# Moving two start-up loads of a fused attention and MLP kernel to the sync queue: wk's last chunks between x2 and x3, and x of group 1 behind x3

## The chip, the cores and the metric

One core of a Trainium2 chip. The metric is the device time of one execution in microseconds (us). A profile's span is 1.7 to 2.1 us shorter than the time of the same execution. All times inside a trace below count from the start of its span. Runs that are compared are "fast" (granted TensorE clock about 1.0) unless the text says otherwise. A single untimed look has the state "unknown".

## The reference

Two branches read the layer norm of the same `x` (2048 tokens, 640 features), and their sum is added to `x`:

```python
xn = layernorm(x)                                   # per token, over 640 features
# branch A: linear attention, 32 heads of 20
q, k, v = split(xn @ wqkv)                          # wqkv 640 x 1920
pq, pk = phi(q), phi(k)                             # phi(t) = t + 1 if t > 0 else exp(t)
o = (pq @ (pk^T @ v)) / (pq . sum(pk))              # per head
A = o @ wo
# branch B
B = gelu(xn @ w1 + b1) @ w2 + b2                    # 640 -> 1536 -> 640
out = x + A + B
```

## The kernel before

The tokens are 16 tiles of 128 (x0 to x15); a group is four tiles. `wk` is the middle third of `wqkv`, in five chunks of 128 rows. Only the start matters here. The loads stand first:

```python
    def load_x(t0, t1, queue=nc.sync):
        queue.dma_start(out=x_all[:, t0:t1, :], in_=xv[:, t0:t1, :])

    def load_wk(k0, k1):
        nc.scalar.dma_start(out=wqk[:, k0:k1, D : 2 * D], in_=wqkv_v[:, k0:k1, D : 2 * D])

    load_x(0, 1)                 # sync (SP) queue
    load_x(1, 2, nc.scalar)      # scalar (ACT) queue
    load_x(2, 3)
    load_x(3, 4)
    # ... cut ...
    load_wk(0, 3)                # ACT queue
    load_wk(3, NC)               # ACT queue; NC = 5
    load_x(4, 8, nc.scalar)      # group 1, four tiles
```

Each partition holds 16 consecutive tokens, so one tile of x is 1280 contiguous bytes of a partition, and x4 to x7 together are 5120 contiguous bytes. A chunk of wk is 1280 bytes of a partition.

The loads of w1, Q's weights and x8 to x15 stand on the sync queue and are held back by a memset on VectorE that follows the statistics of x1 (cut). Then comes the compute, in program order for each engine:

```python
    nc.scalar.preload_act_table_set("natural_log_exp_and_others")
    emit_warm(10)                # ten matmuls on constants, before any data is there
    emit_stats(0)                # VectorE: bn_stats of two halves of 320 columns, then bn_aggr
    emit_center(0)               # VectorE: x0 - mean (its rstd is applied later)
    emit_T_first(0, ((0, 3, nc.scalar.copy), (3, NC, nc.scalar.copy)))   # PE, copies on ScalarE
    emit_warm(1)
    emit_stats(1)
    emit_later_loads()
    emit_stats(2)
    emit_rstd(0, 2)              # ScalarE: Ln, Exp
    emit_norm(1)                 # VectorE
    emit_Ka(0)                   # PE: K of x0, five matmuls over the chunks of wk
    emit_rstd(2, 3)
    emit_T_first(1, ((0, 3, nc.scalar.copy), (3, NC, nc.scalar.copy)))
    emit_stats_half(3, 0)
    emit_norm(2)
    emit_stats_half(3, 1)
    emit_Kb(0)
    emit_T(2, nc.vector.tensor_copy, (0, 3, NC))
    emit_Ka(1, 0, 3)
    # ... cut: K of x1, x2, x3 ...
    for j in range(NJ):
        emit_h(0, j)             # PE: h = xn @ w1, the first long unbroken piece of TensorE work
        # ... cut ...
```

The lines of the profile that recur: L342 and L352 are the matmuls of K, L286 the transposes of x0 and x1, L261 the transposes of x2 and x3, L530 the matmuls of h, L227 the statistics, L247 the norm.

## Time and profile before

| | before |
|---|---|
| time, median of 3 runs | 196.26 us (196.21 to 197.03) |
| span of the profiled run | 194.4 us |
| PE busy | 188.7 us, 97% |
| first matmul of h | 13.57 us |

TensorE (PE) is the bottleneck. Lines of the page: the busy times, and the head of the chain that ended last.

```profile
PE 188.7 (97%) x1229; PEld 111.2 (57%) x1240; DVE 163.3 (84%) x392; ACT 89.8 (46%) x165; POOL 21.3 (11%) x54
...
PE 94%; DMA 3%; ACTq 0%; issue 0%; DVE 0%
```

Read: to the end of the kernel hardly anything but matmuls stands in the chain. What can still be moved is the moment at which the unbroken work begins. The chain in order of time (start, length, what) shows which load is in it:

```profile
1.73 5.83 DMA wqk<-in_A_wqkv_dram
7.56 0.04 issue
7.60 0.59 PE bank_169 L342 x2
8.19 0.17 PE bank_177 L286 x3
8.36 0.11 PE bank_182 L286 x2
8.47 0.28 PE bank_191 L352 x5
8.75 0.33 PE bank_197 L261 x5
```

It is wk's second piece, chunks 3 and 4. The timeline of PE at the same place (start, busy us, what, and in brackets the idle time before it with what ended it):

```profile
6.39 0.82 PE L342 MATMUL bank_169<-wqk,xnT 128*128 128x512 bf16 x3 [0.24 <-ACT xnT L290]
7.60 0.59 PE L342 MATMUL bank_169<-wqk,xnT 128*128 128x512 bf16 x2 [0.39 <-DMA wqk<-in_A_wqkv_dram]
8.03 0.33 PE L286 MATMUL bank_177<-identity,xn 128*128 128x128 bf16 x3
8.20 0.27 PE L286 MATMUL bank_182<-identity,xn 128*128 128x128 bf16 x2
8.31 0.44 PE L352 MATMUL bank_191<-wqk,xnT 128*128 128x128 bf16 x5
8.63 0.45 PE L261 MATMUL bank_197<-identity,xn 128*128 128x128 bf16 x5
```

The first K product does three chunks, waits 0.39 us for the load, and does the last two. That wait is what the change goes for. VectorE (DVE) is without a pause there. These are its lines around the two norms (L247) that the next transposes need:

```profile
7.43 0.40 DVE L247 TENSOR_SCALAR xn<-x_all,mv,rstd 128x640 bf16<-128x640 bf16 x1
7.74 0.49 DVE L227 BATCH_NORM_STATS2 stats<-x_all 128x6 f32<-128x320 bf16 x1
8.14 0.43 DVE L247 TENSOR_SCALAR xn<-x_all,mv,rstd 128x640 bf16<-128x640 bf16 x1
```

The norm of x2 ends at 8.14 + 0.43 = 8.57, and its transpose (L261) starts at 8.63. So there are two things that can hold the transpose of x2, at almost the same moment: the load, through PE's own order, and VectorE's chain.

### The profile page before, as it was taken

The page shows a single profiled execution, that of the slowest core. Times are in us where ns is not written, and L with a number is a line of the kernel's source. Part 1 is how long each engine was busy: PE and PEld are TensorE (multiplying, and loading weights), DVE is VectorE, ACT ScalarE, POOL GpSimd, SP SyncE. Part 2 cuts the span into 40 slices and gives each one's busy share as a digit, 9 for nine tenths or more (in the row PEclk, how much of TensorE's full clock was granted, in tenths as well). Part 3 has the DMA queues.
Part 4 walks back from the last instruction along what each step waited for, and adds up shares of the span by engine and source line. Part 5 has one row for each costly group of instructions (what it writes and reads, how often), then busy time and mean ns, then how long its engine had stood idle before and what let it go on. Part 6 is the DMA issues. An engine that isn't in the chain of part 4 may idle for free.

```text
span 194.4 us, 3333 instructions
## 1 busy us (share of the span) xinstructions
PE 188.7 (97%) x1229; PEld 111.2 (57%) x1240; DVE 163.3 (84%) x392; ACT 89.8 (46%) x165; POOL 21.3 (11%) x54
## 2 busy tenths in 40 slices
PE   8799999999999999999999999999999999999993
PEld 2464444544445454444445777767777777777772
DVE  2978969999699998696878999899999999777442
ACT  2569676558679688899795230050011010110100
POOL 1004170003239100002400100000000000000000
PEclk9999999999999999999999999999999999999999
DMA  6999735944343000000009885300201021010112
GB/s 196 347 251 348 279 81 107 343 182 100 102 122 84 0 0 2 0 0 3 0 4 230 290 245 172 112 0 2 71 0 67 0 71 58 11 67 3 67 58 77
DMA packets 24447, 20.19 MB, mean 104 GB/s; under 512 B 11120, under 2 KB 24048, under 8 KB 24432
## 3 DMA queue, kind: packets, MB, share of 16 engines
q1 hardware_dynamic: 23328, 18.20, 30.8%
q10 hardware_dynamic: 1104, 1.80, 2.5%
q8 instruction: 9, 0.15, 0.3%
q14 instruction: 6, 0.05, 0.1%
HBM read 12.78 MB, written 5.24 MB: 93 GB/s over the span
## 4 chain that ended last, share of the span: by engine, by line
PE 94%; DMA 3%; ACTq 0%; issue 0%; DVE 0%
DMA wqk<-in_A_wqkv_dram 3%; PE bank_1282 L884 2%; PE bank_1273 L884 2%; PE bank_1209 L851 2%; PE bank_2112 L1037 1%; PE bank_2028 L1037 1%; PE bank_1944 L1037 1%; PE bank_1860 L1037 1%; PE bank_1771 L1037 1%; PE bank_1682 L1037 1%; PE bank_1556 L1037 1%; PE bank_1434 L1037 1%; PE bank_1398 L884 1%; PE bank_1386 L884 1%; PE bank_1510 L1037 1%; PE bank_1580 L1037 1%
## 5 line engine op out<-in xcount | busy, mean ns | idle before, releaser
L1037 PEld LDWEIGHTS <-xn 128*128 128x128 f16 x198 | 19.0, 98 | 7.2
L530 PEld LDWEIGHTS <-w_91 128*128 128x128 bf16 x120 | 11.7, 98 | 13.9
L227 DVE BATCH_NORM_STATS2 stats<-x_all 128x6 f32<-128x320 bf16 x32 | 13.7, 469 | 2.9 <-DMA x_all<-in_A_x_dram 2.9
L518 PEld LDWEIGHTS <-wqk 128*128 128x128 bf16 x100 | 9.7, 98 | 11.1
L342 PEld LDWEIGHTS <-xnT 128*128 128x128 bf16 x80 | 7.2, 98 | 7.3 <-issue 0.7
L884 PEld LDWEIGHTS <-xn 128*128 128x128 bf16 (+1 forms) x80 | 7.8, 98 | 3.0
L247 DVE TENSOR_SCALAR xn<-x_all,mv,rstd 128x640 bf16<-128x640 bf16 x16 | 6.2, 436 | 3.7 <-POOL rstd L243 3.6
L946 DVE TENSOR_TENSOR pqT<-pqT,xnT 128x256 bf16<-128x256 bf16 (+1 forms) x30 | 8.5, 328 | 0.0
L682 PEld LDWEIGHTS <-w_91 128*128 128x128 bf16 (+1 forms) x48 | 4.6, 97 | 5.6 <-issue 0.3
L352 PEld LDWEIGHTS <-xnT 128*128 128x128 bf16 x80 | 5.8, 98 | 3.5
L1052 PEld LDWEIGHTS <-Sq 128*128 128x128 f16 x66 | 6.3, 98 | 2.5 <-DVE Sq L937 0.2
L451 DVE TENSOR_TENSOR x_all<-x_all,b2b 128x640 bf16<-128x640 bf16 x16 | 7.0, 480 | 0.0
L190 POOL TENSOR_SCALAR_AFFINE_SELECT emask<-emask 128x160 int8<-128x160 int8 (+3 forms) x20 | 6.7, 346 | 0.9
L302 DVE TENSOR_SCALAR pqT<-pqT 128x512 bf16<-128x512 bf16 x20 | 5.7, 285 | 0.6 <-ACT pqT L299 0.6
L1052 PEld LDWEIGHTS <-pqT 128*128 128x128 bf16 x50 | 4.8, 98 | 1.8
L1037 PEld LDWEIGHTS <-hT_79 128*128 128x128 bf16 x48 | 4.7, 98 | 1.7
L1037 PEld LDWEIGHTS <-hT_80 128*128 128x128 bf16 x48 | 4.7, 98 | 1.7
L1132 ACT CAST late<-bank_1486 128x320 bf16<-128x320 f32 x1 | 0.4, 425 | 10.4 <-PE bank_1489 L1128 10.4
L216 PE MATMUL bank_124<-const-bfloat16-1.0 128*128 128x512 bf16 x10 | 4.2, 605 | 0.8 <-PEq L1280 0.8
L937 DVE TENSOR_TENSOR Sq<-pqT 128x256 f16<-128x256 bf16 x16 | 4.3, 284 | 0.0
L783 DVE TENSOR_TENSOR pk<-pk,GT 128x512 bf16<-128x512 bf16 x10 | 4.2, 422 | 0.0
L682 PEld LDWEIGHTS <-wv 128*128 128x128 f16 x24 | 2.2, 97 | 3.2 <-issue 0.7
(647 smaller groups left out, 508.5 us busy)
## 6 DMA issues: line engine op xcount, KB each, us to landing
xnT<-rec_rows SPq DMA_DIRECT2D x20, 128.0 KB, 2.6
out_dram<-late SPq DMA_DIRECT2D x14, 160.0 KB, 1.8
w_91<-in_B_w_dram SPq DMA_DIRECT2D x2, 960.0 KB, 7.8
w_93<-in_B_w_dram SPq DMA_DIRECT2D x3, 640.0 KB, 7.9
x_all<-in_A_x_dram SPq DMA_DIRECT2D x2, 640.0 KB, 8.5
wqk<-in_A_wqkv_dram SPq DMA_DIRECT2D x1, 800.0 KB, 8.1
wv<-in_A_wqkv_dram SPq DMA_DIRECT2D x1, 800.0 KB, 6.3
woA<-in_A_wo_dram SPq DMA_DIRECT2D x5, 160.0 KB, 3.0
```

The costliest lines, as they stand in the source:

```text
L190: nc.gpsimd.affine_select(out=out, in_=out, compare_op=ALU.is_ge, fill=0.0, base=base, pattern=pattern, channel_multiplier=sign)
L227: nc.vector.bn_stats(out=st[:, half, :], in_=x_all[:, t, half * HALF : (half + 1) * HALF])
L247: nc.vector.tensor_scalar(out=xn[:, t, ds], in0=x_all[:, t, ds], scalar1=mv[:, t, 0:1], scalar2=rstd[:, t : t + 1], op0=ALU.subtract, op1= ...
L342: nc.tensor.matmul(K_ps[t][:], lhsT=xnT[:, k, t * P : (t + 1) * P], rhs=wqk[:, k, D : D + TOK], start=(k == 0), stop=(k == NC - 1),)
L451: nc.vector.tensor_tensor(out=x_all[:, t, :], in0=x_all[:, t, :], in1=b2b[:], op=ALU.add)
L518: nc.tensor.matmul(ps[:], lhsT=wqk[:, k, m * P : (m + 1) * P], rhs=xnT[:, k, gs], start=(k == 0), stop=(k == NC - 1),)
L530: nc.tensor.matmul(ps[:], lhsT=w1[:, k, j * P : (j + 1) * P], rhs=xnT[:, k, g * TOK : (g + 1) * TOK], start=(k == 0), stop=(k == NC - 1),)
L682: nc.tensor.matmul(self.ps[name][:], lhsT=left[:, c, js], rhs=x_block(*block, c) if block else Tx({4: 3, 5: 0, 6: 1, 7: 2}[p], c), start=( ...
L884: nc.tensor.matmul(ps if len(right.shape) == 3 else ps.rearrange("p (c n) -> p c n", c=NC), lhsT=left[:, t, self.i], rhs=right[:, t], star ...
L946: nc.vector.tensor_tensor(out=pqT[:, c, gs], in0=pqT[:, c, gs], in1=xnT[:, c, gs], op=ALU.mult)
L1037: nc.tensor.matmul(self.ps[name][:, cols], lhsT=left[:, j], rhs=right[:, j, cols], start=(start and j == 0), stop=False, skip_group_check= ...
L1052: nc.tensor.matmul(self.ps[name][:, cols], lhsT=left[:, c], rhs=right[:, c, cols], start=False, stop=(stop and c == CH - 1), skip_group_ch ...
```

## The change

Its intent: wk's last chunks go ahead of x3, so that the first K product finds them. x4 to x7 follow behind x3 on the sync queue, and no wait is added to hold them back ("ungated").

```diff
-    def load_wk(k0, k1):
-        nc.scalar.dma_start(out=wqk[:, k0:k1, D : 2 * D], in_=wqkv_v[:, k0:k1, D : 2 * D])
+    def load_wk(k0, k1, queue=nc.scalar):
+        queue.dma_start(out=wqk[:, k0:k1, D : 2 * D], in_=wqkv_v[:, k0:k1, D : 2 * D])

     load_x(0, 1)
     load_x(1, 2, nc.scalar)
     load_x(2, 3)
+    load_wk(3, NC, nc.sync)
     load_x(3, 4)
+    load_x(4, 8)
 ... (cut)
     load_wk(0, 3)
-    load_wk(3, NC)
-    load_x(4, 8, nc.scalar)
```

The compute instructions and their order on PE, VectorE, ScalarE and GpSimd are the same in both kernels.

## The prediction

> **What bounds the kernel now.** The page gives PE 188.7 of 194.4 us busy (97%). The chain of waits is PE 94%, DMA 3%: one DMA, the second piece of wk (chunks 3 and 4, 320 KB), then matmuls back to back to the end. So only the first 14 us can move.
>
> **The start, from the timeline and the landings of the DMA issues (us).**
>
> | load | queue, issued | landed | first needed | slack |
> |---|---|---|---|---|
> | x0 | SP 0.81 | 3.85 | stats 3.87 | 0 |
> | x1 | ACT 0.80 | 4.08 | 5.34 | 1.3 |
> | wk chunks 0-2 | ACT 1.23 | 5.87 | 6.39 | 0.5 |
> | x2 | SP 1.25 | 4.40 | 6.38 | 2.0 |
> | x3 | SP 1.71 | 6.18 | 7.74 | 1.5 |
> | wk chunks 3-4 | ACT 1.73 | 7.56 | about 7.2 | -0.39 |
> | x4-7 | ACT 2.27 | 9.18 | 13.22 | 4.0 |
> | w1, first half | SP 6.51 | 12.97 | 13.52 | 0.55 |
>
> The one late load is wk 3-4: PE waits 0.39 us for it at 7.60. VectorE has no such hole: from x0's landing until 9.67 it never waits for a DMA.
>
> **What the change does.** It adds no compute and no bytes. wk 3-4 goes ahead of x3, x4-7 move from the ACT to the SP queue. The transfers still share the same engines: the windows show about 390 GB/s at 4 to 5 us, and 387 at 9 to 10 us, where the SP queue works alone. That agrees with the Trainium skill, "DMA: Bandwidth & Descriptors", "Issuing engines are not separate DMA queues"; I expect no bandwidth, only another order. Between 4.0 and 4.5 us no packet of SP's queue moves, although x3 was issued at 1.71; the transfers go nearly in order of issue.
>
> wk 3-4 now has 1280 KB up to its end instead of 1440: 160 KB at 390 GB/s is 0.4 us (estimate), so it lands at about 6.7 to 7.15 and the 0.39 us wait goes. x3 takes the place that wk 3-4 had, 1440 KB, so lands at about 7.5 instead of 6.2: 0.2 us before VectorE wants it. wk 0-2 may land up to 0.4 later (6.3), still before 6.39. x4-7 land at about 9.2 as before; w1's first half about 13.0.
>
> **How much is critical.** Little. After the wait, the transposes of x1 need its norm (VectorE, 7.43 to 7.83; weight load at 7.88, itself waiting for it), matmuls at 8.03: at most 0.11 us comes forward. Then the transpose of x2 needs the norm that ends at 8.57, and starts at 8.63 already. So the wait of 0.39 us turns into waits on VectorE, which this change does not move. Left over: 0.02 to 0.1 us out of 196. ScalarE's table load comes 1 us earlier, for nothing: its first work, at 5.86, waits for PE.
>
> **Prediction:** 196.2 us, 195.7 to 196.9; faster by over 2%: 0.01, within 2%: 0.97, slower: 0.02.
>
> **What would show it right.** The DMA wait of PE at 7.6 is gone; transposes of x1 near 7.92, of x2 at 8.6 again, now released by VectorE; first matmul of h (w1) at 13.5 within 0.1 of 13.57; the chain of waits passes through DVE and x0 instead of wk.
>
> **What would make it wrong.** x3 later than 7.8: VectorE's third-tile statistics stand before the norm of x2, so PE is late by the same amount (0.1 to 0.5 us slower). wk 0-2 later than 6.39. w1's first half behind x4-7 on the same queue later than 13.5. The runs before spread by 0.8 us, more than the effect; nothing here reaches 2% (3.9 us).

## The result

| | before | change |
|---|---|---|
| time, 6 runs each | 196.38 us (195.99 to 197.03) | 196.36 us (196.07 to 196.47) |
| ratio, with 95% interval | | 0.9992 (0.9973 to 1.0011) |
| span of the profiled run | 194.4 us | 194.4 us |

A ratio is the mean time of one kernel's fast runs over that of the other's of the same rounds, so not quite the ratio of the medians. The change is worth nothing that the runs resolve. In the trace it did what it was meant to do. Landing times (us, the completion of each load in the trace's DMA records):

| load | before | change | needed at |
|---|---|---|---|
| x0 | 3.85 | 3.81 | at once |
| wk chunks 0-2 | 5.87 | 5.70 | 6.4 |
| wk chunks 3-4 | **7.56** | **6.57** | 7.2 |
| x3 | **6.18** | **6.99** | 7.7 |
| x4 to x7 | 9.18 | 8.57 | 13.2 |
| w1, first half | 12.97 | 11.87 | 13.5 |

PE's timeline after the change, the lines that answer to those of before:

```profile
6.51 1.25 PE L342 MATMUL bank_169<-wqk,xnT 128*128 128x512 bf16 x5
7.84 0.34 PE L286 MATMUL bank_177<-identity,xn 128*128 128x128 bf16 x3
8.02 0.28 PE L286 MATMUL bank_182<-identity,xn 128*128 128x128 bf16 x2
8.13 0.44 PE L352 MATMUL bank_191<-wqk,xnT 128*128 128x128 bf16 x5
8.59 0.45 PE L261 MATMUL bank_197<-identity,xn 128*128 128x128 bf16 x5
```

The five matmuls of the first K product now run in one piece. The transposes of x1 come 0.19 us sooner (8.03 to 7.84), but the transpose of x2 only 0.04 (8.63 to 8.59). The weight loads of TensorE (PEld) say what they waited for:

```profile
7.83 0.28 PEld L286 LDWEIGHTS <-xn 128*128 128x128 bf16 x5 [0.57 <-DVE xn L247]
8.07 0.32 PEld L352 LDWEIGHTS <-xnT 128*128 128x128 bf16 x5
8.58 0.28 PEld L261 LDWEIGHTS <-xn 128*128 128x128 bf16 x5 [0.19 <-DVE xn L247]
```

Both transposes wait for VectorE's norms (L247). VectorE's own lines stand where they stood, 0.04 us sooner, as x0 landed 0.04 sooner:

```profile
7.39 0.40 DVE L247 TENSOR_SCALAR xn<-x_all,mv,rstd 128x640 bf16<-128x640 bf16 x1
7.70 0.49 DVE L227 BATCH_NORM_STATS2 stats<-x_all 128x6 f32<-128x320 bf16 x1
8.10 0.43 DVE L247 TENSOR_SCALAR xn<-x_all,mv,rstd 128x640 bf16<-128x640 bf16 x1
```

And the chain has changed its head. The load of wk is gone from it; x0 and VectorE are in it:

```profile
0.81 3.00 DMA x_all<-in_A_x_dram
3.81 0.02 issue
3.83 0.90 DVE stats L227 x2
...
7.26 0.21 DVE mv L229
7.47 0.32 DVE xn L247
7.79 0.05 issue
7.84 0.34 PE bank_177 L286 x3
```

The first matmul of h starts at 13.51 instead of 13.57 us. From there to the end of the span both traces take 180.86 us. The matmuls, compared one by one, are 0.06 to 0.07 us earlier in the change than before, from 9.8 us to the last.

### The profile page after: what moved, and what is told of

Same layout as the page of the kernel before. It is cut to its first block, busy times and chain, and to the rows that moved or that the text cites. A ratio compares the mean times of both kernels' runs of the same rounds, so it can differ in the third digit from the quotient of the medians.

```text
span 194.4 us, 3333 instructions
## 1 busy us (share of the span) xinstructions
PE 189.4 (97%) x1229; PEld 111.4 (57%) x1240; DVE 163.3 (84%) x392; ACT 89.8 (46%) x165; POOL 21.7 (11%) x54
## 3 DMA queue, kind: packets, MB, share of 16 engines
HBM read 12.78 MB, written 5.24 MB: 93 GB/s over the span
## 4 chain that ended last, share of the span: by engine, by line
PE 94%; DVE 2%; DMA 2%; issue 1%
PE bank_1282 L884 2%; PE bank_1273 L884 2%; PE bank_1209 L851 2%; DMA x_all<-in_A_x_dram 2%; PE bank_2112 L1037 1%; PE bank_2028 L1037 1%; PE bank_1944 L1037 1%; PE bank_1860 L1037 1%; PE bank_1771 L1037 1%; PE bank_1682 L1037 1%; PE bank_1556 L1037 1%; PE bank_1434 L1037 1%; DVE stats L227 1%; PE bank_1398 L884 1%; PE bank_1386 L884 1%; PE bank_1510 L1037 1%
## 5 line engine op out<-in xcount | busy, mean ns | idle before, releaser
L247 DVE TENSOR_SCALAR xn<-x_all,mv,rstd 128x640 bf16<-128x640 bf16 x16 | 6.2, 435 | 3.7 <-POOL rstd L243 3.6
```

Source lines behind the costliest of these rows:

```text
L247: nc.vector.tensor_scalar(out=xn[:, t, ds], in0=x_all[:, t, ds], scalar1=mv[:, t, 0:1], scalar2=rstd[:, t : t + 1], op0=ALU.subtract, op1= ...
```

## The experiments

Theory A: PE starts its unbroken work when the last of a few things is there. Before, these were wk 3-4 and VectorE's chain from x0, almost together; the change removes the first and leaves the second. What comes after h is fixed, so every delay or gain at h counts in full.

Rival B: the whole wait of 0.39 us is gained near 7.6 us and lost again later, for example at w1, which is now behind x4 to x7 on the same queue.

Rival C: the start is not critical at all; a hole there is absorbed later.

Twelve runs were made, of ten new kernels (e8 is e4 again) and of the change itself (e7). In the edits, "before" and "change" name the kernel that was edited. The first four ran on one chip, the next four on another, then three, then one. Each set ran beside runs of the kernel before, with which it is compared; e3 and e4 are single looks.

### e1: wk 3-4 later (from before)

```diff
     load_wk(0, 3)
-    load_wk(3, NC)
     load_x(4, 8, nc.scalar)
+    load_wk(3, NC)
```

> Kernel before with its last two loads of the ACT queue exchanged: x4-7, then wk 3-4. Theory A (PE starts its unbroken work when the last of two things is there, wk 3-4 or VectorE's norms; behind that every delay counts in full): wk 3-4 lands about 9.2 us instead of 7.56, the first matmul of h starts at about 13.57 + 1.6 = 15.2, the time is 1.4 to 1.8 us longer, about 198.0 (+0.8%). Rival C (the start is not critical; a hole there is absorbed later): wk lands as late, but the time stays within 0.3 us of before.

Measured: 197.28 us (4 runs), ratio to before 1.0048 (1.0033 to 1.0063). wk 3-4 landed at 8.65, not 9.2, so the size is less than expected.

```profile
6.64 0.82 PE L342 MATMUL bank<-wqk,xnT 128*128 128x512 bf16 x3 [0.24 <-ACT xnT L290]
8.69 0.59 PE L342 MATMUL bank<-wqk,xnT 128*128 128x512 bf16 x2 [1.23 <-DMA wqk<-in_A_wqkv_dram]
```

The wait is 1.23 us, h starts at 14.67 and the rest of the span takes 180.83 us: the loss of 1.09 us at h is a loss of 1.06 us in the span. Rival C falls. From the landing of wk 3-4 to h it is 14.67 - 8.65 = 6.02 us here, and 13.57 - 7.56 = 6.02 us before.

### e2: x3 later (from the change)

```diff
     load_wk(3, NC, nc.sync)
-    load_x(3, 4)
     load_x(4, 8)
+    load_x(3, 4)
```

> Changed kernel with x3 behind x4-7 on the sync queue. Theory A: x3 lands at about 8.6 us instead of 7.0; VectorE wants it at 7.70, so its statistics start about 0.9 later, the norm of x2 and the transpose of x2 come 0.9 later (about 9.5), the first matmul of h at about 14.4 instead of 13.51, the time is 0.7 to 1.0 us longer (about 197.2). It would show that x3 has only 0.7 us of room in the change, and that a loss on VectorE counts in full. Rival C: time within 0.3 us.

Measured: 197.28 us (4 runs), ratio to before 1.0044 (1.0027 to 1.0060). x3 landed at 8.72 and VectorE waited for it:

```profile
7.32 0.40 DVE L247 TENSOR_SCALAR xn<-x_all,mv,rstd 128x640 bf16<-128x640 bf16 x1
8.75 0.49 DVE L227 BATCH_NORM_STATS2 stats<-x_all 128x6 f32<-128x320 bf16 x1 [1.03 <-DMA x_all<-in_A_x_dram]
9.16 0.43 DVE L247 TENSOR_SCALAR xn<-x_all,mv,rstd 128x640 bf16<-128x640 bf16 x1
```

h started at 14.57 (14.4 was expected of A), and the loss of 1.06 us at h reached the end in full (1.08 us of the span). Here PE's own loads were in time, and VectorE alone made the loss.

### e3: the first half of the change alone

wk 3-4 on the sync queue between x2 and x3; x4 to x7 stay on the ACT queue.

```diff
     load_wk(3, NC, nc.sync)
     load_x(3, 4)
-    load_x(4, 8)
 ...
     load_wk(0, 3)
+    load_x(4, 8, nc.scalar)
```

> The first half of the change alone: wk 3-4 on the sync queue between x2 and x3; x4-7 stay on the ACT queue behind wk 0-2. If transfers go nearly in order of issue, x4-7 are now issued at about 1.75 on ACT, together with wk 3-4 and before x3: wk 3-4 and x4-7 share, wk 3-4 lands later than in the change (7.0 to 7.6 instead of 6.57), and x3 lands last, at 8 to 8.6 instead of 6.99, which makes VectorE late by 0.4 to 0.9 us; first matmul of h at 13.9 to 14.4. That would say why the change moves x4-7 too. If the queues shared evenly whatever the order of issue, x3 would land at about 7.5 and h start at 13.5.

Measured: 198.75 us (one look, state unknown). wk 3-4 landed at 8.60 and x3 at 8.87, later than in either kernel and than expected (7.0 to 7.6, and 8 to 8.6). What the two queues moved between 6 and 7 us (packets, MB, share of the engines; q1 is the sync queue, q10 the ACT queue):

```profile
q10 hardware_dynamic: 63, 0.32, 80.9%
q1 hardware_dynamic: 64, 0.08, 22.0%
```

Packet for packet the queues take turns in this window, 63 to 64. But a packet, which in these traces is one contiguous run, has 5 KB in x4 to x7 and 1.25 KB in wk or x3, so x4 to x7, which nobody needs before 13.2 us, get four bytes for each byte of the urgent loads. The equal turns agree with the Trainium skill, "DMA: Bandwidth & Descriptors", section "Queues, rings and completion order": an engine goes round the queues packet by packet. The page's packet is several descriptors, typically 9 to 17; whether the turns here have that unit no run shows. Nor are turns equal at all times: from 4 to 4.5 us of the kernel before, all 155 packets are of the ACT queue, although x3 had been issued on the sync queue at 1.71.

The loss of time is larger than the landings explain: wk 3-4 at 8.60 + 6.02 gives h at 14.6, x3 at 8.87 + 5.84 gives 14.7, but h started at 16.20. The remaining 1.5 us go with the clock. In the windows below (stretch, its length, busy time of PE, PEld, DVE, ACT, POOL, then PEclk, the granted clock), cut at the clock changes that the trace records:

```profile
5.28:8.69 3.41, 1.54 (x10) 0.70 (x11) 2.75 (x10) 1.65 (x6) 0.00 (x0) 1.00 0.99 325
8.69:12.11 3.42, 3.42 (x20) 2.25 (x20) 2.29 (x8) 1.73 (x5) 0.00 (x0) 0.50 1.15 299
```

After a window of 3.41 us with PE busy for 1.54 us, the next 3.42 us run at half clock with PE busy throughout, which is worth up to 1.7 us (an estimate: half of 3.42). So here the wait was paid for twice. Its length alone does not decide that: e1 waited 1.23 us, longer than the 1.11 us here, in a window with 1.90 us of work, and kept its clock.

### e4 and e8: the second half of the change alone, looked at and then timed

x4 to x7 on the sync queue behind x3; wk 3-4 stays on the ACT queue.

```diff
     load_x(3, 4)
+    load_x(4, 8)
 ...
     load_wk(3, NC)
-    load_x(4, 8, nc.scalar)
```

> The second half of the change alone: x4-7 on the sync queue behind x3, wk 3-4 still on ACT behind wk 0-2. wk 3-4 and x4-7 are issued about the same time (1.73 and 2.15), so wk 3-4 lands at 7.0 to 7.7 as before, PE waits 0 to 0.5 us for it, x3 at about 6.2 as before, first matmul of h at 13.5 to 13.65, one time within 0.3 us of before.

Measured: 200.09 us (one look, state unknown). The expectation of "no change" was wrong: wk 3-4 landed at 10.31, PE waited 3.0 us for it, and half clock followed from 9.57 to 12.98; h started at 17.51.

> The second half alone (x4-7 to sync, wk 3-4 left on ACT) once more, timed: the first look gave 200.09 with wk 3-4 landing at 10.31. If that comes from the two loads alternating packet by packet (x4-7 in packets of 5 KB, wk in packets of 1.25 KB), it repeats: wk 3-4 lands after 9 us in this run too and the time is 199 to 200.2. If it was an accident of one run, wk 3-4 lands at 7.5 to 8.5 and the time is 196.3 to 197.3.

Measured: four runs of 197.12, 197.19, 199.31 (fast) and 201.04 (slow; the profiled one), ratio of the fast runs to before 1.0067 (1.0020 to 1.0113). It lies between the two expectations. In the profile wk 3-4 landed at 10.17, so the late landing did repeat. In the two runs near 197.15 it was probably earlier: their span, 195.4 us, less 180.86 leaves h at about 14.5, and less 6.02 a landing at about 8.5 (an estimate, if wk was the limit there; those runs have no trace). Between 6 and 7 us the queues' packets were not one to one here, and from 8 to 10 us wk's queue moved almost nothing:

```profile
q1 hardware_dynamic: 421, 0.66, 92.9%
q10 hardware_dynamic: 7, 0.01, 1.1%
```

Why the last few packets of wk trickle like this is not settled. That this half alone is slower than both kernels, and uneven from run to run, is shown by the fast runs alone.

### e5: x0 in two halves, in the kernel before

```diff
-    load_x(0, 1)
-    load_x(1, 2, nc.scalar)
+    nc.sync.dma_start(out=x_all[:, 0, 0:HALF], in_=xv[:, 0, 0:HALF])
+    nc.scalar.dma_start(out=x_all[:, 0, HALF:D], in_=xv[:, 0, HALF:D])
+    load_x(1, 2)
     load_x(2, 3)
```

> Kernel before, with x0 fetched as two halves of 320 columns, one on each queue, and x1 on sync behind it, so that x0 is there sooner: landed about 3.5 us instead of 3.85, and VectorE's chain (statistics, norms of x1 and x2) about 0.3 us sooner. Theory A (before, PE waits for wk 3-4; in the change, for VectorE's chain from x0): wk 3-4 still lands at about 7.5, PE still waits for it, longer than before (0.6 to 0.8 instead of 0.39 us), the first matmul of h stays at 13.4 to 13.6, time within 0.2 us of before. Rival B (the gain is made at 7.6 and lost later, at w1 or another load): the same here; it is told apart by the next run.

Measured: 197.40 us (6 runs), ratio to before 1.0048 (1.0026 to 1.0070). A miss: the edit was not clean. x0 did land at 3.20 and 3.37, but x3 was now issued beside x4 to x7 of the other queue, took turns with its large packets and landed at 8.98 instead of 6.18:

```profile
9.00 0.49 DVE L228 BATCH_NORM_STATS2 stats<-x_all 128x6 f32<-128x320 bf16 x1 [1.43 <-DMA x_all<-in_A_x_dram]
```

h started at 14.82. As a test of A against B it says little, but it repeats e2 from another side: h is 14.82 - 8.98 = 5.84 us behind the landing of x3, and 14.57 - 8.72 = 5.85 us in e2. It also repeats e3: the urgent small load beside the large one is the one that loses.

### e6: the same edit in the change

> The same edit of x0 in the changed kernel. Theory A: nothing but VectorE's chain holds PE there, so 0.3 us sooner at x0 is 0.2 to 0.35 us sooner at the transpose of x2 (8.25 to 8.4 instead of 8.59) and at the first matmul of h (13.15 to 13.3 instead of 13.51); time 0.2 to 0.3 us under the change (0.1 to 0.15%, at the edge of what the runs resolve; the trace decides). Rival B: the transposes come sooner but h starts at 13.5 again, with a wait in between.

Measured: 196.31 us (6 runs), ratio to before 0.9985 (0.9965 to 1.0005); h at 13.50. No gain, another miss of the design: x1, now second on its queue beside wk 0-2, landed at 5.24 instead of 3.99, and VectorE lost in front of x1 what it had gained at x0.

```profile
5.26 0.89 DVE L228 BATCH_NORM_STATS2 stats<-x_all 128x6 f32<-128x320 bf16 x2 [0.45 <-DMA x_all<-in_A_x_dram]
```

In the change without this edit the statistics of x1 start at 5.29. The start of h follows VectorE again: 13.50 against 13.51.

### e7: the change again

Edit: none.

> The changed kernel as it is, once more, for its spread and for runs on the same chip beside the two before: 196.2 to 196.5, ratio to before 0.999 to 1.000. The trace shows whether the landings (wk 3-4 at 6.57, x3 at 6.99) and the start of h (13.51) repeat within 0.1 us, and whether the moment at which the clock of TensorE is let up (4.6 in before's trace, about 6.4 in the change's) moves from run to run without regard to the kernel.

Measured: 196.10 us (6 runs, 195.89 to 196.25), ratio to before 0.9977 (0.9957 to 0.9997). Landings: x0 3.76, wk 3-4 6.63, x3 7.02; h at 13.47. The landings and h repeat within 0.1 us. From the landing of x0 to h it is 9.70 us, as in the change's first profile (13.51 - 3.81). The clock of TensorE was let up at 4.0 us here, at 6.5 in the first profile of the change and at 4.7 in that of before, with the same ten matmuls ahead of it, so this moment does not belong to the kernel. (A warm-up matmul takes 0.63 us before that moment and 0.38 us after it.)

The two ratios of the change, 0.9992 and 0.9977, have overlapping intervals. The traces account for 0.03 to 0.06% (0.06 to 0.11 us at h), so at most a small part of the second is shown as a gain.

### e9 and e10: VectorE's chain shortened, no load touched

The mean and variance of x1 are taken from its first 320 columns alone, in before (e9) and in the change (e10). (The start of w1's load, which waits for these statistics, comes 0.36 and 0.19 us sooner; w1 is not waited for in either trace.) This is a wrong computation; the outputs still passed the comparison with the reference, as rstd and mean of half a row are close to those of the row.

```diff
     emit_warm(1)
-    emit_stats(1)
+    st1 = small.tile([P, 2, nc.vector.BN_STATS_DIM], F32, name="stats")
+    nc.vector.bn_stats(out=st1[:, 0, :], in_=x_all[:, 1, 0:HALF])
+    nc.vector.bn_aggr(out=mv[:, 1, :], in_=st1[:, 0:1, :])
```

> Kernel before with no load touched, but VectorE's chain shortened by one statistics instruction (about 0.40 us): the mean and variance of x1 are taken from its first 320 columns alone, so the result is wrong on purpose (slightly). Theory A: PE waits for wk 3-4 at about 7.6 as before; the norm of x1 then comes about 0.24 sooner (ScalarE's copies before rstd bound it) and is not what PE waits for; the transpose of x2 starts at 8.6 behind PE's own work, the first matmul of h at 13.45 to 13.6: no gain, time within 0.2 us of before.

Measured: 195.99 us (6 runs, 195.90 to 196.24), ratio to before 0.9976 (0.9958 to 0.9994); h at 13.30. The expectation (no gain, wk waits) was wrong. The loads are those of before, but in this run wk 3-4 landed at 7.15 instead of 7.56, and PE did not wait for it:

```profile
6.45 1.33 PE L342 MATMUL bank<-wqk,xnT 128*128 128x512 bf16 x5 [0.24 <-ACT xnT L290]
```

So the 0.39 us of the first profile is not a fixed property of the kernel before: the same loads land up to 0.4 us apart, on both sides of the moment at which they are needed.

> The same shortened statistics (wrong on purpose) in the changed kernel, loads as in the change. Theory A (after the change PE waits for VectorE's chain): the norm of x1 about 0.24 sooner, transposes of x1 at 7.5 to 7.65 instead of 7.8, the transpose of x2 at 8.3 to 8.4 instead of 8.55, first matmul of h at 13.2 to 13.3 instead of 13.46 to 13.51; time 0.2 to 0.3 us under the change. If something else bounds the start (ScalarE's copies, w1), h starts at 13.4 or later here too.

Measured: 196.27 us (6 runs), ratio to before 0.9999 (0.9976 to 1.0023); h at 13.44, the transpose of x2 at 8.52. The absolute values missed, as x0 landed late in this run, at 4.04 instead of 3.8. Counted from the landing of x0, as in the table below, the chain is 0.30 us shorter, as expected. The times of these two runs decide nothing; the traces do.

| trace | x0 landed | first matmul of h | difference |
|---|---|---|---|
| before | 3.85 | 13.57 | 9.73 |
| change | 3.81 | 13.51 | 9.70 |
| change again (e7) | 3.76 | 13.47 | 9.70 |
| before, half statistics (e9) | 3.90 | 13.30 | 9.40 |
| change, half statistics (e10) | 4.04 | 13.44 | 9.40 |

(The differences are formed before rounding.) The lines behind the third column are, in this order, h in before and in the change, then VectorE's first instruction on x0 and h in e9, and the same two in e10:

```profile
13.57 1.24 PE L530 MATMUL bank_268<-xnT,w_91 128*128 128x512 bf16 x5
13.51 1.24 PE L530 MATMUL bank_268<-xnT,w_91 128*128 128x512 bf16 x5
3.92 0.89 DVE L227 BATCH_NORM_STATS2 stats<-x_all 128x6 f32<-128x320 bf16 x2 [2.96 <-DMA x_all<-in_A_x_dram]
13.30 1.89 PE L530 MATMUL bank<-xnT,w 128*128 128x512 bf16 x8
4.06 0.89 DVE L227 BATCH_NORM_STATS2 stats<-x_all 128x6 f32<-128x320 bf16 x2 [3.09 <-DMA x_all<-in_A_x_dram]
13.44 1.89 PE L530 MATMUL bank<-xnT,w 128*128 128x512 bf16 x8
```

This is what decides. With 0.40 us less work on VectorE, h comes 0.30 us sooner after x0 in both kernels, to 0.01 us alike. VectorE's chain from x0 sets the start of h in the change; in the kernel before it does so too when wk 3-4 is in time, as in e9, while in the first profile of before wk 3-4 came last, by 0.03 us. That 0.10 of the 0.40 us does not arrive is probably ScalarE: in e9 it ends rstd at 7.09 and the norm of x1 starts at 7.13, where before 0.40 us lay between the two (7.03 and 7.43). No run tests this. The landing of x0 itself, 3.75 to 4.16 us in the traces that load it whole, moves h by more than the change does. Rival B falls too: h moves with the chain, and from h to the end of the span it is 180.83 to 180.86 us in all five traces.

### e11: x0 and x1 in two halves each (from the change)

```diff
-    load_x(0, 1)
-    load_x(1, 2, nc.scalar)
+    for t in (0, 1):
+        nc.sync.dma_start(out=x_all[:, t, 0:HALF], in_=xv[:, t, 0:HALF])
+        nc.scalar.dma_start(out=x_all[:, t, HALF:D], in_=xv[:, t, HALF:D])
     load_x(2, 3)
```

> The changed kernel with x0 and x1 each fetched as two halves of 320 columns, one on each queue, ahead of everything else; a correct kernel, meant to shorten VectorE's chain at its head without the mistake of the last try (x1 behind x0 on one queue against wk 0-2 landed 1.2 us late). x0 lands at about 3.2, x1 at 3.9 to 4.2, so VectorE is 0.5 sooner and does not wait for x1. wk 0-2 is issued 0.45 later and lands at 5.7 to 6.2 (needed at about 5.9), wk 3-4 at 6.6 to 7.1 (needed at about 6.5), x3 at 7.0 to 7.5 (needed at about 7.1): three limits meet, so of the 0.5 us 0.1 to 0.4 are left at the first matmul of h (13.1 to 13.4); time 196.0 to 196.3, under the change by at most 0.2%.

Measured: 198.97 us median of 6 runs (196.90, 196.98, 198.82 and 199.12 fast, 199.86 and 200.30 slow), ratio of the fast runs to before 1.0075 (1.0030 to 1.0119). A failure. x0 and x1 landed early (3.2 to 3.8), but wk 0-2 was issued 0.5 us later, met wk 3-4 on the other queue and landed at 8.07 instead of 5.7. PE waited 2.6 us for it, and half clock followed.

### e12: the statistics of x1 on ScalarE (from the change)

A correct kernel that keeps the change's loads. ScalarE has nothing to do from 3.0 to 6.0 us.

```diff
     emit_warm(10)
+    sq1 = consts.tile([P, 2], F32, name="sq1")
+    dump = hT[0][:, 0:2, :].rearrange("p j n -> p (j n)")
+    nc.scalar.activation(out=dump[:, 0:D], in_=x_all[:, 1, :], func=ACT.Identity, scale=1.0 / D, accum_out=mv[:, 1, 0:1])
+    nc.scalar.activation(out=dump[:, 0:D], in_=x_all[:, 1, :], func=ACT.Square, scale=D ** -0.5, accum_out=sq1[:, 0:1])
+    nc.gpsimd.tensor_tensor(out=sq1[:, 1:2], in0=mv[:, 1, 0:1], in1=mv[:, 1, 0:1], op=ALU.mult)
+    nc.gpsimd.tensor_tensor(out=mv[:, 1, 1:2], in0=sq1[:, 0:1], in1=sq1[:, 1:2], op=ALU.subtract)
     emit_stats(0)
 ... (cut)
-    emit_stats(1)
     emit_later_loads()
     emit_stats(2)
-    emit_rstd(0, 2)
+    emit_rstd(0, 3)
     emit_norm(1)
+    emit_norm(2)
     emit_Ka(0)
-    emit_rstd(2, 3)
     emit_T_first(1, ((0, 3, nc.scalar.copy), (3, NC, nc.scalar.copy)))
-    emit_stats_half(3, 0)
-    emit_norm(2)
-    emit_stats_half(3, 1)
+    emit_stats(3)
```

> A correct kernel, loads as in the change: the statistics of x1 move from VectorE to ScalarE, which has nothing to do between 3.0 and 6.0 us (two activations with accumulated sums, of x and of its square; two small GpSimd operations make the variance), one rstd serves x0 to x2, and the norms of x1 and x2 follow each other. Theory A (h starts at the landing of x0 + 9.70 us because VectorE works without a hole from there to the norm of x2; two half-statistics runs gave + 9.40 for 0.40 us less on VectorE): the norms of x1 and x2 end near 7.6 and 8.0, the transpose of x2 starts at 8.15 to 8.3 instead of 8.55, h at the landing of x0 + 9.3 to 9.45 (13.1 to 13.25 at the usual 3.8), time 195.8 to 196.05, 0.1 to 0.2% under the change. If h starts later than + 9.6, ScalarE's sums or the copies behind them have become the limit instead.

Measured: 196.05 us median of 6 runs (195.71 to 197.90), ratio to before 0.9999 (0.9960 to 1.0038): no better kernel shown. In its profile VectorE's norms ended at 8.1 us although x0 landed late (4.01), so the chain was shortened, even with a new wait of 0.67 us for ScalarE's rstd in it. But most of the loads were late in this run, and PE waited for wk 0-2 (landed at 6.69 instead of 5.7) in place of VectorE; then w1's first half landed at 13.42, and h started just behind it, at 13.47:

```profile
6.73 1.24 PE L342 MATMUL bank<-wqk,xnT 128*128 128x512 bf16 x5 [0.42 <-DMA wqk<-in_A_wqkv_dram]
```

With VectorE out of the way, two other loads are the next limits: PE waited 0.42 us for the first, and h about 0.1 us for the second (the last K product starts 0.39 us ahead of h here, 0.28 in before). Whether their lateness belongs to this kernel or to this one run is open. Still, h came 9.46 us after x0, 0.24 sooner than 9.70. From h to the end this trace takes 180.57 us, 0.28 less than the others; why was not looked into.

## Why the prediction was right

- **The time.** Predicted 196.2 us (195.7 to 196.9) and within 2%; measured 196.36, and 196.10 in the second set of six. Any kernel that costs what the one before costs falls into this range, so the time alone tests little; the trace does.
- **The wait of PE for wk goes.** Right: no wait for that load in either trace of the change. It landed at 6.57 and 6.63.
- **The wait turns into one on VectorE.** Right, and this is the step on which the prediction rests. The transposes of x1 started at 7.84 and 7.79 (predicted 7.92), that of x2 at 8.59 and 8.54 (predicted 8.6), released by the norms. The half-statistics pair shows the cause and not only its trace: 9.70 falls to 9.40 us in both kernels when VectorE has less to do.
- **What is left over, 0.02 to 0.1 us.** Right: h 0.06 us sooner in the profiled pair. The two limits before were 3.85 + 9.70 = 13.55 (x0 and VectorE) and 7.56 + 6.02 = 13.57 (wk 3-4). Taking the second away could give 0.03 us; the other 0.04 is the earlier landing of x0 in that run, which the change did not make. So more than half of the 0.06 us is luck.
- **The landings.** Direction right for wk 3-4 and x3 alone, sizes off. wk 3-4 was said to come 0.4 us sooner and came 0.98 sooner, x3 at about 7.5 and it was 6.99, wk 0-2 "up to 0.4 later" and it was 0.17 sooner, w1 at 13.0 and it was 11.87. The estimate took all bytes ahead at a fixed rate and the one profile as typical; e9, with the same loads as before, had wk 3-4 at 7.15, so that profile was the later of two samples.
- **"The transfers go nearly in order of issue".** Only half right, and harmless in this change alone. It held where one queue had the small loads to itself. Where x4 to x7 are in flight on the other queue (e3, e5), the packets take turns and the small loads fall behind. The prediction did not see that both halves of the change are needed together: each alone costs time (e3 in one look, e8 in fast runs).

Is the change at least steadier? Of all 46 runs of the kernel before, 11 are above 196.6 us, of the 12 runs of the change none. But of the 12 runs of e10 and e12, which have the change's loads, four are above 196.6 too, and of the six of e9, with the loads of before, none. So a load of wk that is now and then late is not shown to be the cause of the slower runs; their cause is open.

## What to carry to other kernels

A wait of 0.39 us in front of the bottleneck engine is worth only the distance to the next thing that would have held it, here 0.03 us; find that thing in the trace before moving a load, by asking when the following instructions had their other inputs. When loads are spread over two queues, look at the size of their contiguous runs: a bulk load of large packets on one queue takes most of the bytes from a small urgent load on the other, so keep the bulk behind the urgent load on the same queue. Even that is no guarantee: in the kernel before, x4 to x7 stood behind wk 3-4 on one queue, and from 6.5 to 7.5 us only 18 of that queue's 97 packets were under 2 KB, the rest already those of x4 to x7, while the last of wk landed at 7.56. Count moments from the landing that starts the chain, not from the start of the span: 9.70 against 9.40 us was clear in three traces against two, while the times of dozens of runs could not show it.

## What the Trainium skill lacked or had wrong

- "DMA: Bandwidth & Descriptors", "Issuing engines are not separate DMA queues" says that issuing from several engines saves only the sequencer's time. For the total rate the traces agree (397 GB/s between 4 and 4.5 us before with only the ACT queue moving; 411 GB/s between 6 and 7 us in the change with only the sync queue; 403 GB/s in the same window of e3 with both). It lacks that the choice of queue and the order on it decide which load lands late: with the same bytes, wk 3-4 landed at 6.57 (change), 7.15 and 7.56 (loads of before), 8.60 (e3) and 10.2 to 10.3 us (e4, e8).
- The same page, "Queues, rings and completion order", has the round by packets, which e3 shows for one window (63 packets to 64). It lacks what follows from it for bytes: 0.32 MB to 0.08 MB, as the packets had 5 KB and 1.25 KB.
- "TensorE: Matmul & The Clock Gate", "Part 1: The HAM clock gate (the "warmup" mystery)" says that the clock falls to half after at least one idle window of about 3.4 us. The length agrees (stretches of 3.41 us at 0.50, e3), an idle window does not: the clock fell after windows of 3.41 us in which PE was busy for 1.54 us (e3), 1.10 (e4), 1.38 (e11) and 1.75 us (e8, a slow run), the longest waits for a load in the first two being 1.1 and 3.0 us. It stayed up after windows with 1.90 us (e1) and 2.35 us (before) of work. That the windows run free of the kernel agrees: the clock was let up at 4.0, 4.7 and 6.5 us.
